# First block of an attention and GeGLU kernel: one statistic, one normalisation, one copy and the order of the up products

## The chip, the cores and the metric

The kernel runs on one core of one Trainium2 chip. The metric is the device time of one execution in microseconds (us). A core has TensorE (PE in the profile; PEld is its weight load), VectorE (DVE), ScalarE (ACT), GpSimd (POOL) and SyncE (SP, which here only issues transfers).

## The reference

```python
xn = layernorm(x)                                   # x: 1 x 2048 x 448, bf16
q, k, v = split(xn @ wqkv)                          # 16 heads of 28
p = softmax(mask(q @ k.T * 28 ** -0.5))             # causal, the last 256 positions
attn = (p @ v) @ wo
ffn  = (gelu_tanh(xn @ w_gate) * (xn @ w_up)) @ w_down    # inner width 1792
out  = x + attn + ffn
```

## The kernel before

The 2048 rows are 16 tiles of 128, worked on in four blocks (qb = 0 to 3) of four tiles. A block has an attention stage of steps (eight in the first block, two for each of four groups of four heads), then a stage that computes the gate products with Gelu. The program's order on each engine is written out by hand: every engine runs its own instructions in the order in which the Python code issues them, and waits for others by semaphores. A step of attention is: scores on TensorE (L680) into the score buffer, of which there is one, four PSUM banks large; the Exp of the whole buffer on ScalarE (L685, 1.88 us); masking; and then a list of other work, `plan[i]`, that is issued behind the step. At steps 4 and 6 the product with v of groups 0 and 1 (`pv`, L654) is issued ahead of the scores; it takes two PSUM banks `ov`, which ScalarE copies (L637) and VectorE adds to (L639).

The other four PSUM banks (b0 to b3) are handed out from a list, `spare`: `take` takes the bank at its head, `give` puts a bank at its end when the instruction that empties it has been issued, and whoever takes the bank later waits for that instruction.

The pieces of work that matter here:

- `stat(t)` (L155, L156), VectorE: mean and variance of a tile. `rstd(t, n)` (L160, L161), ScalarE: reciprocal deviation of n tiles, two small instructions. `norm(t)` (L170), VectorE: the normalised tile; for tiles from 4 on it is two instructions, of 448 and 64 columns. `dma_transp(t)` (L184): a transposing transfer from SP's queue into `xnT`.
- `v_dense` and `v_half` compute v of a tile in the first block, `v_copy` (L234) brings it from PSUM to `v_sb`, on the engine that is passed to it.
- `gen_qk()` yields the q and k products of groups 1 to 3 of the first block, nine items: for a group, q, k, and a last item that adds the remaining 64 rows and casts q (L251, ScalarE) and k (L252, VectorE) to SBUF. Group 3's q is an item of its own behind group 2's k.
- `gen_up(0, (1, 2, 3, 0, 4), (2, 3, 4))` (L497) computes the up products of five pairs of the first block's feed-forward part ahead of time: a pair is seven items (chunks of the contraction) of two matmuls each into two banks `ue`; behind the last item both are copied to `hT` (L514), both on VectorE, or for pairs 2, 3 and 4 the second on ScalarE. It reads `xsw`, the other half order of `xnT`, and `wu`.
- `gen_pairs(1, ...)` computes v (L331) and q and k (L345) of the second block. It needs `xnT` of tiles 4 to 7, `wvs` (loaded at L808), `xsw` of tiles 4 to 7 (`swap`, L478, a transfer from `xnT`: tiles 4 and 5 in one pair of transfers, tiles 6 and 7 in another) and `wsq` (`swap_weights`, L484).
- `masked` (L611), GpSimd, masks the first four steps; `fill_pads` (L295 to L307), GpSimd, fills columns of the weights which `swap_weights` then copies. `scale_o` (L620) runs on GpSimd, too.

`(u, 3)` in a plan means three items of the generator `u = chain(gen_qk(), gen_up(...))`, 44 items in all: nine of q and k, 35 of up products. The plan's first steps and what they call:

```python
def ahead():          # behind step 0
    norm(4); dma_transp(4)
    # two loads of wvs, SP's queue
def ahead2():         # within step 1
    stat(6); stat(7); rstd(5, 3)
def ahead3():         # within step 2
    for t in (5, 6, 7): norm(t); dma_transp(t)
    swap(1, 4, 2); fill_pads(False); swap_weights(); swap(1, 6, 2)
    # loads of wg, wu, x_sb, wo, wd
plan = [[last_v, (u, 3), ahead], [(u, 2), ahead2, (u, 2)], [(u, 1), ahead3, (u, 7)], [(u, 10), lambda: stat(8)],
        [lambda: stat(9), (u, 11), lambda: fill_pads(True)], [(u, 8), "sums"], ...]
```

So step 0's three items are group 1's q and k and their casts; step 1 holds group 2's q, k, group 3's q and group 2's casts; step 2 holds group 3's k and casts and six of the seven chunks of the first pair. Step 3 (ten items) ends the first pair, does the second, and begins the third with two chunks. `rstd(4, 1)` has been issued long before, ahead of step 0. Ahead of step 0 come also the v copies: `v_copy(0)` on ScalarE, `v_copy(1)` and `v_copy(3)` on VectorE; `last_v` computes v of tile 2 and copies it on VectorE.

Of the kernel before, what the change touches and what calls it, by code (L numbers as in the profile page):

```python
# [27 lines left out]
def kernel(  # L28
# [11 lines left out]
    nc = tc.nc  # L40
# [112 lines left out]
    def stat(t):  # L153
        st = work.tile([P, nc.vector.BN_STATS_DIM], f32, name="st")
        nc.vector.bn_stats(out=st[:, :], in_=x_sb[:, t, :])  # L155
        nc.vector.bn_aggr(out=mv_all[:, t, :], in_=st[:, :])  # L156

    def rstd(t, n):
        lnv = work.tile([P, 4], f32, name="lnv")
        nc.scalar.activation(out=lnv[:, 0:n], in_=mv_all[:, t:t + n, 1], func=ACT.Ln, bias=eps_t[:, 0:1], scale=1.0)  # L160
        nc.scalar.activation(out=rstd_all[:, t:t + n], in_=lnv[:, 0:n], func=ACT.Exp, scale=-0.5)  # L161
# [3 lines left out]
    def norm(t):  # L165
        xn = work.tile([P, 4, P], bf16, name="xn", bufs=4)
        xf = xn[:, :, :].rearrange("p a b -> p (a b)")
        both = ((0, D, 0), (D, 64, 384))
        for lo, n, src in both if t > 3 else both[:1]:
            nc.vector.tensor_scalar(out=xf[:, lo:lo + n], in0=x_sb[:, t, src:src + n], scalar1=mv_all[:, t, 0:1],  # L170
                                    scalar2=rstd_all[:, t:t + 1], op0=ALU.subtract, op1=ALU.mult)
        xns[t] = xn
# [9 lines left out]
    def dma_transp(t):  # L182

        nc.sync.dma_start_transpose(out=xnT[:, :, t * P:(t + 1) * P], in_=xns.pop(t)[:, :, :].rearrange("p a b -> p (a b)"))  # L184
# [26 lines left out]
    def take(name, cols=QB, tag=None):  # L211

        tag = tag or spare[0]
        spare.remove(tag)
        ps = psum.tile([P, QB], f32, name=name, tag=tag, bufs=1)[:, 0:cols]
        held[id(ps)] = tag, ps
        return ps  # L220

    def give(*tiles):
        for ps in tiles:
            spare.append(held.pop(id(ps))[0])


    def v_dense(t, pv, first=True):
        mm3(pv, lambda c: xnT[:, c, t * P:(t + 1) * P], lambda c: wv[:, c, :], first, not first)
# [4 lines left out]
    def v_copy(t, pv, copy):  # L233
        copy(out=v_sb[:, t, :, 0:Dh], in_=pv.rearrange("p (h d) -> p h d", d=Dh))  # L234
        give(pv)
# [52 lines left out]
    def fill_pads(last):  # L288


        def put(dst, src, n, lo):

            src = src.rearrange("p (j d) -> p j d", d=Dh)[:, :, lo:]
            if n == 4:
                nc.gpsimd.tensor_copy(out=dst[:, 12:16, Dh:32], in_=src[:, :, 24:28])  # L295
            src = src[:, :, 0:24].rearrange("p j (g i) -> p g j i", i=8)[:, :, :, 0:4]
            nc.gpsimd.tensor_copy(out=dst[:, 0:12, Dh:32].rearrange("p (g j) i -> p g j i", j=4), in_=src)

        if not last:
            for c in range(3):  # L300
                k = wraw[:, c, D + 12 * Dh:2 * D]
                put(wqp[:, c, :, :], k, 4, 0)
                put(wkp[:, c, :, :], k, 3, 4)
            return
        put(w3p[0:64, :, :], w3k[0:64, :], 4, 0)
        put(w3p[64:128, :, :], w3k[64:128, :], 3, 4)
        nc.gpsimd.memset(w3p[64:128, 12:16, :], 0.0)  # L307
# [161 lines left out]
    def new_hT(qb):  # L469
        hT = blk.tile([P, NF, QB], bf16, name="hT", tag="hT")  # L470
        hTs[qb] = hT
# [269 lines left out]
    def pads(eng, dst, gs):  # L741

        hs = slice(4 * gs.start, 4 * gs.stop)
        c0 = D * (dst is wkp)
        src = wraw[:, 0:3, c0 + Dh * hs.start:c0 + Dh * hs.stop]
        eng(out=dst[:, :, hs, 0:Dh], in_=src.rearrange("p c (h d) -> p c h d", d=Dh))
# [20 lines left out]
    pvs = [take("pv", D)]  # L767
# [25 lines left out]
    qk_copies(0, 0, pq, pk)  # L793
    pads(nc.vector.tensor_copy, wqp, slice(1, 2))
    v_copy(0, pvs[0], nc.scalar.copy)
    v_copy(1, pvs[1], nc.vector.tensor_copy)
    pads(nc.vector.tensor_copy, wkp, slice(1, 2))
    v_dense(3, pvs[3], False)
    v_copy(3, pvs[3], nc.vector.tensor_copy)
# [1 line left out]
        pads(nc.vector.tensor_copy, dst, slice(2, 4))  # L801

    def ahead():
        norm(4)
        dma_transp(4)
        wv64 = A_wqkv[0:3 * P, 2 * D:3 * D].rearrange("(c h p) n -> h p c n", h=2, p=64)
        for hi in range(2):
            nc.sync.dma_start(out=wvs[64 * hi:64 * hi + 64, :, :], in_=wv64[1 - hi])  # L808

    def ahead2():  # L810
        stat(6)
        stat(7)
        rstd(5, 3)

    def ahead3():
        for t in (5, 6, 7):
# [18 lines left out]
    for qb in range(NB):  # L835
        if qb in (1, 3):
            tc.mark_branch_hint_location("general", hint="LikelyTaken",
                                         engines=[mybir.EngineType.DVE if qb == 1 else mybir.EngineType.PE])
        early = ()
        if qb == 0:  # L840
            new_hT(0)
            early = (0, 1, 2, 3, 4)
            def last_v():
                v_dense(2, pvs[2], False)
                v_copy(2, pvs[2], nc.vector.tensor_copy)

            u = chain(gen_qk(), gen_up(0, (1, 2, 3, 0, 4), (2, 3, 4)))
            w = gen_pairs(1, (("v", 0), ("v", 2), ("k", 0), ("k", 1), ("k", 2)))
            plan = [[last_v, (u, 3), ahead], [(u, 2), ahead2, (u, 2)], [(u, 1), ahead3, (u, 7)], [(u, 10), lambda: stat(8)],
                    [lambda: stat(9), (u, 11), lambda: fill_pads(True)], [(u, 8), "sums"],  # L850
                    [(w, 7), "inverse", "scale", (w, 7), lambda: stat(10), (w, 3)],
                    [(w, 4), lambda: stat(11), lambda: rstd(8, 4), (w, 7), "masks", "sums", (w, 7), "inverse"]]
        else:
            d = gen_down(qb - 1)
            if qb < 3:
                u = gen_pairs(qb + 1, (("v", 0), ("k", 0), ("v", 2), ("k", 1), ("k", 2)))
                plan = [[(d, 14)], [(d, 11)], [(d, 11)], [(u, 7)], [(d, 17)], ["sums", (d, 1), (u, 7), "inverse"], [(u, 11)],
                        [lambda: q_last(qb + 1, nc.vector.tensor_copy), (d, 6), "sums"], [(d, 2), "inverse", (d, 9)],
                        [(u, 9), "masks", (u, 1)]]
                plan[3] = [(d, 1), (u, 7)]  # L860
                if qb == 2:
                    plan[0], plan[2] = [(d, 13)], [(d, 10)]
                if qb == 1:
                    for i, j in enumerate((0, 1, 2, 2)):
                        plan[j].insert(0, lambda t=12 + i: stat(t))
                    plan[4].append(lambda: rstd(12, 4))
                    plan[1] = plan[1][:1] + [lambda: q_last(1, nc.vector.tensor_copy), (d, 8)]
                    plan[2] = plan[2][:2] + [(d, 12), lambda: collect(1)]
                    plan[4].append(lambda: deliver(1))
            else:  # L870
                new_hT(3)
                early = (1, 2, 3, 4, 5, 6)
                u = gen_up(3, early, (4, 5, 6))
                plan = [[(u, 12)], [(u, 9)], [(d, 12)], [(d, 10)], [(d, 12)], [(d, 1), (u, 7), "sums"], [(d, 12), "inverse"],
                        ["sums", "inverse", (d, 11)], [(d, 11)], [(d, 1), "masks", (u, 13), "masks", (u, 1)]]
        if qb in (1, 2):
            swap(qb + 1)
        score_pool(1)
        rest, after, flush = attention(qb, plan)
        nc.scalar.preload_act_table(ACT.Gelu_apprx_tanh)  # L880
        score_pool(2)
        if qb not in hTs:
            new_hT(qb)

        def hook(f):
            after(f)
            if qb in (1, 2) and f == 0:
                collect(qb + 1)
            if f == (8, 2, 2, 0)[qb]:
                o_collect(qb, nc.sync if qb else nc.scalar)  # L890
            if f == (12, 4, 4, 0)[qb]:
                o_deliver(qb)
                o_finish(qb)
            if qb == 0 and f == 6:
                nc.gpsimd.tensor_copy(out=wo[64:128, 3, :], in_=wo[0:64, 3, :])
            if qb in (1, 2) and f == 10:
                deliver(qb + 1)
            t = ({0: 8, 4: 9, 8: 10, 10: 11} if qb == 0 else {4: 12, 6: 13, 8: 14, 10: 15} if qb == 1 else {}).get(f)
            if t is not None:
                norm(t)  # L900
                dma_transp(t)

        gated(qb, early, rest, flush, hook)
        if qb < NB - 1:
            nc.scalar.preload_act_table_set("natural_log_exp_and_others")
# [159 lines left out]
```

## Time and profile before

| | |
|---|---|
| median of 3 runs | 212.45 us (212.22 to 212.5) |
| profiled execution | 212.49 us, of which span 210.7 us |
| granted TensorE clock | 1.0 |
| busy: PE, DVE, ACT, POOL | 205.3, 156.7, 134.2, 43.9 us |
| Exp of attention (L685) | 38 of 1.879 us |
| first block, scores of step 0 | 11.28 us from the span's start |
| first block, scores of step 7 | 32.82 us |

Times in a timeline are microseconds from the start of the span. A row gives the start, the duration, the engine, the line of the kernel, the operation, what is written and read, and the count when several instructions are drawn together; in brackets stands how long the engine had been idle and which instruction released it. A matmul's duration contains its pipeline, so that matmuls overlap in the rows, and the pace is read from their starts; some records of matmuls are missing. SP's rows are the issuing of transfers, not their landing.

### The profile page before, as it was taken

What the parts mean: (1) busy time and instruction counts of PE and PEld (TensorE: products, weight loads), DVE (VectorE), ACT (ScalarE), POOL (GpSimd) and SP (SyncE); (2) the same over time, 40 slices, a digit from 0 to 9 for tenths busy, and PEclk for the clock granted to TensorE, in tenths of its full rate; (3) what the DMA queues carried; (4) which work ended last, traced back from release to release, by engine and by line L of the source; (5) the groups of instructions that cost most, each with busy time, mean ns of one, the idle gap of its engine ahead of it and who ended that gap; (6) DMA issues with size and microseconds to landing.
All of it is one profiled execution on the core that took longest, in us unless ns stands there. A gap on an engine that the chain in (4) does not pass through costs nothing. (4 is left out here: it accounts for less than half of the span.)

```text
span 210.7 us, 6666 instructions
## 1 busy us (share of the span) xinstructions
PE 205.3 (97%) x2837; PEld 99.5 (47%) x2842; DVE 156.7 (74%) x360; ACT 134.2 (64%) x131; POOL 43.9 (21%) x87
## 2 busy tenths in 40 slices
PE   7999999999999999999999999999999999999994
PEld 2444454544444445444445444544444454544572
DVE  6899889899788985696538897395385699696532
ACT  4688896966777977413778688623587787756000
POOL 5388912260000220040000112013000023042000
PEclk9999999999999999999999999999999999999999
DMA  6999979969411001003331000100000010100011
GB/s 186 282 228 164 132 189 228 249 193 230 110 46 49 25 0 41 10 0 68 62 91 47 25 3 23 23 3 19 24 5 0 3 47 5 44 11 14 3 47 50
DMA packets 24890, 15.68 MB, mean 74 GB/s; under 512 B 9208, under 2 KB 24728, under 8 KB 24856
## 3 DMA queue, kind: packets, MB, share of 16 engines
q1 hardware_dynamic: 23814, 14.87, 31.8%
q10 hardware_dynamic: 1042, 0.34, 1.0%
q8 instruction: 23, 0.38, 0.7%
q14 instruction: 11, 0.09, 0.3%
HBM read 9.26 MB, written 2.41 MB: 55 GB/s over the span
## 5 line engine op out<-in xcount | busy, mean ns | idle before, releaser
L685 ACT ACTIVATE p_sb<-sc 128x2048 bf16<-128x2048 f32 x38 | 71.4, 1879 | 17.0 <-PE sc L680 11.4
L537 ACT ACTIVATE p_sb<-gt 128x1024 bf16<-128x1024 f32 x28 | 28.7, 1025 | 31.3 <-PE gt L497 29.7
L620 POOL TENSOR_TENSOR oN<-oc,l 128x512 bf16<-128x512 f32 x16 | 20.7, 1300 | 122.9 <-DVE l L633 122.9
L497 PE MATMUL gt<-xnT,wg 64*128 64x512 bf16 x224 | 45.6, 376 | 0.0
L406 PE MATMUL po<-wd,hT 128*128 128x448 bf16 (+1 forms) x224 | 44.7, 347 | 0.0
L497 PE MATMUL gt<-xsw,wg 64*128 64x512 bf16 x168 | 40.7, 376 | 0.0
L605 DVE TENSOR_TENSOR p_sb<-p_sb,masks 128x256 bf16<-128x256 bf16 (+1 forms) x98 | 30.5, 365 | 7.5 <-ACT p_sb L685 7.5
L547 DVE TENSOR_TENSOR hT<-p_sb,u 128x512 bf16<-128x512 bf16 x34 | 21.7, 675 | 13.3 <-PE u L497 13.3
L406 PEld LDWEIGHTS <-hT 128*128 128x128 bf16 x238 | 21.9, 98 | 19.1 <-issue 2.0
L497 PEld LDWEIGHTS <-wg 64*128 64x128 bf16 x392 | 19.1, 94 | 22.3
L497 PEld LDWEIGHTS <-wu 64*128 64x128 bf16 x392 | 19.2, 94 | 21.9 <-issue 0.7
L497 PE MATMUL u<-xnT,wu 64*128 64x512 bf16 x136 | 28.1, 376 | 0.0
L497 PE MATMUL u<-xsw,wu 64*128 64x512 bf16 x102 | 24.7, 376 | 0.0
L639 DVE TENSOR_TENSOR oc<-oc,ov 128x512 f32<-128x512 f32 (+1 forms) x16 | 10.5, 658 | 10.4 <-ACT oc L637 10.2
L497 PE MATMUL ue<-xnT,wu 64*128 64x512 bf16 x88 | 18.1, 377 | 0.0
L680 PE MATMUL sc<-qT,kT 28*64 28x320 bf16 (+4 forms) x736 | 16.2, 259 | 0.2 <-ACT p_sb L685 0.2
L497 PE MATMUL ue<-xsw,wu 64*128 64x512 bf16 x66 | 16.2, 376 | 0.0
L680 PEld LDWEIGHTS <-kT 28*64 28x64 bf16 x736 | 8.2, 103 | 12.4 <-issue 11.2
L394 DVE TENSOR_TENSOR res<-po,x_sb 128x448 bf16<-128x448 f32 (+1 forms) x14 | 8.1, 605 | 7.9 <-PE po L406 6.7
L514 DVE CAST hT<-ue 128x512 bf16<-128x512 f32 x16 | 10.5, 685 | 2.4 <-PE ue L497 2.4
L637 ACT COPY oc<-ov 128x512 f32<-128x512 f32 x16 | 9.4, 586 | 4.4 <-PE ov L654 4.4
L633 DVE STREAM_TRANSPOSE l<-inv_all 128x512 f32<-128x512 f32 x16 | 11.1, 701 | 0.1
(112 smaller groups left out, 279.9 us busy)
## 6 DMA issues: line engine op xcount, KB each, us to landing
out_dram<-res SPq DMA_DIRECT2D x15, 112.0 KB
wd<-in_B_w_down_dram SPq DMA_DIRECT2D x2, 784.0 KB
x_sb<-in_A_x_dram SPq DMA_DIRECT2D x3, 448.0 KB
xsw<-xnT SPq DMA_DIRECT2D x6, 192.0 KB
wu<-in_B_w_up_dram SPq DMA_DIRECT2D x4, 224.0 KB
wg<-in_B_w_gate_dram SPq DMA_DIRECT2D x2, 448.0 KB
wu<-in_B_w_up_dram SPq DMA_DIRECT2D x2, 336.0 KB
wg<-in_B_w_gate_dram SPq DMA_DIRECT2D x2, 336.0 KB
```

The lines of the kernel that those rows point to most:

```text
L406: nc.tensor.matmul(po[:, 0:w], lhsT=x[:, k, tt * P:(tt + 1) * P], rhs=wt[:, k, lo:up], start=start and n == 0, stop=stop and n == len(term ...
L497: nc.tensor.matmul(ps, lhsT=w[64 * hi:64 * hi + 64, c, p * P:(p + 1) * P], rhs=xchunk(qb, hi, c, qb * QB, QB), start=c == 0, stop=c == 6, ...
L514: copy(out=hTs[qb][:, p + 7 * i, :], in_=us[i])
L537: nc.scalar.activation(out=ges[p][:, :, :], in_=gt[:, :, :], func=ACT.Gelu_apprx_tanh)
L547: nc.vector.tensor_tensor(out=hT[:, p + 7 * i, :], in0=ge[:, i, :], in1=u, op=ALU.mult)
L605: nc.vector.tensor_tensor(out=reg, in0=reg, in1=m, op=ALU.mult)
L620: nc.gpsimd.tensor_tensor(out=oN[:, g, :], in0=oc[:, :], in1=inv, op=ALU.mult)
L633: nc.vector.transpose(out=l1[:, :, :], in_=inv_all[:, 4 * qb + g, :].unsqueeze(2).to_broadcast([P, 16, 32]))
L637: nc.scalar.copy(out=oc[:, :], in_=ov[0][:, :])
L639: nc.vector.tensor_tensor(out=oc[:, q0:], in0=oc[:, q0:], in1=ov[1][:, q0:], op=ALU.add)
L680: nc.tensor.matmul(ss[k0:k0 + nk, j, col:col + nq], lhsT=kT[r, g, kt * P + k0:kt * P + k0 + nk], rhs=qT[r, g, ring(qb).start + q0:ring(qb) ...
L685: nc.scalar.activation(out=p_sb[:, :, 0:ncol], in_=ss[:, :, 0:ncol], func=ACT.Exp, scale=SCALE)
```

## The change

Three things of the first block are moved, and one goes to another engine.

- `v_copy(1)` runs on ScalarE instead of VectorE.
- `stat(6)` is issued behind `last_v` in step 0, ahead of group 1's k cast, instead of in step 1.
- `norm(4)` and `dma_transp(4)` are issued in step 1 behind `rstd(5, 3)`, instead of behind group 1's casts in step 0. The two loads of `wvs` keep their place in step 0, and so come ahead of tile 4's transpose in SP's queue.
- The up products are dealt out as 8, 12 and 9 items to steps 3, 4 and 5 instead of 10, 11 and 8: step 3 ends with the second pair complete, step 4 holds the third pair and five chunks of the fourth, step 5 the rest.

```diff
     v_copy(0, pvs[0], nc.scalar.copy)
-    v_copy(1, pvs[1], nc.vector.tensor_copy)
+    v_copy(1, pvs[1], nc.scalar.copy)
...
     def ahead():
-        norm(4)
-        dma_transp(4)
         wv64 = A_wqkv[0:3 * P, 2 * D:3 * D].rearrange("(c h p) n -> h p c n", h=2, p=64)
         for hi in range(2):
             nc.sync.dma_start(out=wvs[64 * hi:64 * hi + 64, :, :], in_=wv64[1 - hi])

     def ahead2():
-        stat(6)
         stat(7)
         rstd(5, 3)
+        norm(4)
+        dma_transp(4)
...
-            plan = [[last_v, (u, 3), ahead], [(u, 2), ahead2, (u, 2)], [(u, 1), ahead3, (u, 7)], [(u, 10), lambda: stat(8)],
-                    [lambda: stat(9), (u, 11), lambda: fill_pads(True)], [(u, 8), "sums"],
+            plan = [[last_v, lambda: stat(6), (u, 3), ahead], [(u, 2), ahead2, (u, 2)], [(u, 1), ahead3, (u, 7)], [(u, 8), lambda: stat(8)],
+                    [lambda: stat(9), (u, 12), lambda: fill_pads(True)], [(u, 9), "sums"],
```

## The prediction

> **What bounds the kernel now.** I read the page first, then the timelines of TensorE, ScalarE, VectorE and the SP queue over the first 31 us, then the table of stretches for the transfers. On the page:
>
> ```profile
> PE   7999999999999999999999999999999999999994
> ```
>
> This is TensorE's busy share in 40 slices: nines in all but the first and the last. So only a gap that TensorE has can be won, and whatever closes one moves all that follows. A nine hides up to a tenth of a slice, some 0.5 us, and such gaps lie in the first block. TensorE's timeline (start, duration, and in brackets idle time and releaser):
>
> ```profile
> 17.76 0.39 PE L204 MATMUL pk<-xnT,w3p 64*128 64x512 bf16 x1
> 18.08 0.37 PE L497 MATMUL ue<-xnT,wu 64*128 64x512 bf16 x1
> ...
> 19.25 0.38 PE L497 MATMUL ue<-xnT,wu 64*128 64x512 bf16 x1
> 19.86 0.43 PE L680 MATMUL sc<-qT,kT 28*64 28x320 bf16 x24 [0.23 <-ACT p_sb L685]
> 20.22 0.60 PE L497 MATMUL ue<-xnT,wu 64*128 64x512 bf16 x3
> ...
> 22.20 0.37 PE L497 MATMUL ue<-xnT,wu 64*128 64x512 bf16 x1
> 22.90 0.62 PE L654 MATMUL ov<-p_sb,v_sb 64*32 64x320 bf16 x36 [0.33 <-DVE hT L514]
> ...
> 25.99 0.38 PE L497 MATMUL ue<-xnT,wu 64*128 64x512 bf16 x1
> 26.29 0.43 PE L680 MATMUL sc<-qT,kT 28*64 28x320 bf16 x24
> ...
> 30.75 0.51 PE L331 MATMUL pv<-wvs,xsw 64*128 64x448 bf16 x2
> ```
>
> The undisturbed step from a last up product to the next scores is 25.99 to 26.29, 0.30 us. The two disturbed ones are 19.25 to 19.86 (0.61 us, released by the Exp) and 22.20 to 22.90 (0.70 us, released by an hT copy). The excess, 0.31 and 0.40 us, is lost; the bracket shows less, since ends of matmuls are modelled. A third loss is small. Ten pairs of up products start between 20.22 and 22.20, nine steps of 0.22 us; a pair of halves, as narrow, costs the same, so the first up product could follow the q and k halves at 17.76 + 0.22 = 17.98, but starts at 18.08.
>
> What holds the Exp of step 2 is on ScalarE:
>
> ```profile
> 4.88 0.20 ACT L161 ACTIVATE rstd_all<-lnv 128x1 f32<-128x1 f32 x1
> ...
> 10.81 0.54 ACT L234 CAST v_sb<-pv 128x448 bf16<-128x448 f32 x1
> 11.82 1.88 ACT L685 ACTIVATE p_sb<-sc 128x2048 bf16<-128x2048 f32 x1 [0.47 <-DVE v_sb L234]
> ...
> 14.51 1.88 ACT L685 ACTIVATE p_sb<-sc 128x2048 bf16<-128x2048 f32 x1
> 17.02 0.30 ACT L160 ACTIVATE lnv<-mv_all,eps_t 128x3 f32<-128x3 f32 x1 [0.63 <-DVE mv_all L156]
> ...
> 17.46 0.57 ACT L251 CAST qT<-pq 128x512 bf16<-128x512 f32 x1
> 17.92 1.88 ACT L685 ACTIVATE p_sb<-sc 128x2048 bf16<-128x2048 f32 x1
> ...
> 20.40 1.88 ACT L685 ACTIVATE p_sb<-sc 128x2048 bf16<-128x2048 f32 x1
> ```
>
> The Exp of step 1 ends at 14.51 + 1.88 = 16.39, but the reciprocal deviation of tiles 5 to 7 waits 0.63 us for VectorE's statistics; behind it stand group 2's q cast (17.46, over at 18.03: the bank which the first up product at 18.08 takes) and the Exp of step 2 (17.92 to 19.80: what the scores at 19.86 wait for, as the scores have one buffer). VectorE in the same time:
>
> ```profile
> 4.43 0.36 DVE L170 TENSOR_SCALAR xn<-x_sb,mv_all,rstd_all 128x448 bf16<-128x448 bf16 x1
> ...
> 11.15 0.61 DVE L234 CAST v_sb<-pv 128x448 bf16<-128x448 f32 x1
> ...
> 13.02 0.60 DVE L234 CAST v_sb<-pv 128x448 bf16<-128x448 f32 x1
> 14.06 0.69 DVE L252 CAST kT<-pk 128x512 bf16<-128x512 f32 x1 [0.44 <-PE pk L204]
> 14.67 0.85 DVE L170 TENSOR_SCALAR xn<-x_sb,mv_all,rstd_all 128x448 bf16<-128x448 bf16 x2
> 15.43 0.61 DVE L155 BATCH_NORM_STATS2 st<-x_sb 128x6 f32<-128x448 bf16 x1
> ...
> 16.80 0.18 DVE L156 BATCH_NORM_AGGREGATE mv_all<-st 128x2 f32<-128x6 f32 x1
> 16.90 0.66 DVE L252 CAST kT<-pk 128x512 bf16<-128x512 f32 x1
> 17.59 2.10 DVE L170 TENSOR_SCALAR xn<-x_sb,mv_all,rstd_all 128x448 bf16<-128x448 bf16 x6
> 19.61 0.68 DVE L252 CAST kT<-pk 128x512 bf16<-128x512 f32 x1
> 20.64 1.29 DVE L514 CAST hT<-ue 128x512 bf16<-128x512 f32 x2 [0.36 <-PE ue L497]
> ```
>
> It idles 0.44 us ahead of group 1's k cast (14.06), then normalises tile 4 (0.85) and takes the statistics of tiles 6 and 7 from 15.43 to 16.98, 0.78 each. These rows carry the first loss.
>
> **The change, part by part.**
>
> *A v copy to ScalarE.* VectorE loses 0.61 us of work (11.15), some 0.52 between starts, so its queue reaches the v copy of 13.02 at about 12.5, and is free at 13.1 instead of 13.62; that copy's product has by then been done, or it costs at most the 0.44 us of the hole. ScalarE gains an equal of the copy at 10.81, 0.54 us, from 11.25 to 11.79. The Exp of step 0 starts at 11.82 because its scores come then, so the copy lies in that hole: cost nothing, at most 0.05; without the cover 0.45, but TensorE does not wait for this Exp by itself.
>
> *Statistics of tile 6 ahead of group 1's k cast.* One statistic, 0.78 us, into 13.1 to 14.06: fits, by 0.18 us. If it didn't, the k cast would slip by up to 0.3, and the scores that need it come at step 2, over 2 us later; cost nothing.
>
> *Tile 4 behind tile 7.* VectorE goes k cast (to 14.75), statistics of tile 7 (to 15.45), tile 4 (0.85, to 16.3), and is free when group 2's k cast comes (16.90 before, about 16.8 now). So the statistics are in at 15.45, a microsecond before the Exp of step 1 ends. ScalarE then runs from 16.39 without a wait: the two small steps take 17.46 − 17.02 = 0.44, the q cast 0.46, so the Exp of step 2 starts at 17.3, 0.62 sooner, and ends at 19.2. The first up product comes at 17.98 (gain 0.10), the scores of step 3 at 19.25 − 0.10 + 0.30 = 19.45 without waiting (gain 0.31). What is late next there is TensorE itself. Tiles 5 to 7 start some 0.14 sooner, as the k cast, not the deviation, now frees VectorE.
>
> *Up products by pairs.* Two chunks leave step 3, of which one goes to step 4 and one more to step 5 (10, 11, 8 become 8, 12, 9): 44 in both orders, nothing added. Step 3 now ends with the second pair whole and the third not begun, so the banks at the head of the spare list for pv(0) are those of the first pair, not those whose copies begin when TensorE wants them. The loss of 0.40 goes, if the first pair's copies are over. They ran 20.64 to 21.93; 0.41 sooner they end at 21.52, if group 3's k cast (19.61 to 20.29, now 0.14 sooner) is out by 20.23, which is tight by less than 0.1. TensorE arrives at 22.90 − 0.40 − 0.41 − 2 × 0.22 = 21.65. I take 0.06 off for this hand-over, and 0 to 0.3 as its bounds. The scores of step 4 follow after pv(0)'s 0.55, at 22.2, and need the Exp of step 3: it starts 0.54 after its scores (19.86 to 20.40), so now at 20.0, and ends at 21.9, 0.3 in time.
>
> *The queue of SP.* Tile 4's transpose moves behind the two wvs loads:
>
> ```profile
> 15.55 1.32 SPq L184 DMA_TRANSPOSE xnT<-xn  x1
> 16.93 1.26 SPq L808 DMA_DIRECT2D wvs<-in_A_wqkv_dram  x2
> 18.45 4.30 SPq L184 DMA_TRANSPOSE xnT<-xn  x3
> 24.14 1.85 SPq L478 DMA_DIRECT2D xsw<-xnT  x2
> ...
> 27.40 1.28 SPq L478 DMA_DIRECT2D xsw<-xnT  x2
> ```
>
> ```profile
> 19.00:20.00 1.00, 0.78 (x15) 0.37 (x19) 1.00 (x4) 1.00 (x2) 0.28 (x2) 1.00 0.13 15
> 20.00:21.00 1.00, 1.00 (x32) 0.64 (x21) 0.64 (x2) 0.88 (x2) 1.00 (x3) 1.00 0.61 147
> ...
> 29.00:30.00 1.00, 1.00 (x44) 0.58 (x25) 0.97 (x3) 1.00 (x3) 0.00 (x0) 1.00 0.83 202
> 30.00:31.00 1.00, 1.00 (x14) 0.68 (x12) 1.00 (x4) 1.00 (x1) 0.00 (x0) 1.00 0.46 78
> ```
>
> The last column of the table is GB/s of all transfers. The wvs loads read an input and wait for no engine: they went out as soon as the transpose ahead of them was issued (15.55 + 1.32 = 16.87). Now they leave before 16.3; the transpose leaves at 16.3 instead of 15.55, 0.75 later, with nothing behind it until tile 5's at about 18.3. The stake lies further on. The swap copies of tiles 6 and 7 go out at 27.40 to 28.68 and the second v product needs them at 30.75. TensorE would be there at 30.75 − 0.75 = 30.0. The transfers' landing has no row; its bounds are 28.68 and 30.75, and as the queues still move 202 GB/s in 29 to 30 and 78 in the next microsecond I take 30.4. So without a shift of this chain TensorE would wait 0.45 there. The chain starts with the swap at 24.14, released by the transposes. Now the transfers were all but idle at 19 to 20 (15 GB/s), with tile 4's transpose and wvs both issued, and at 147 in the next microsecond: something held wvs until then, and what stood ahead of it was the transpose. With wvs gone ahead, that hole is used, tiles 4 to 7 go back to back, and the swap may leave up to 24.14 − 22.75 = 1.39 sooner, when SP has issued the last transpose. I take about 1; 0.45 is enough. The Trainium skill's "DMA: Bandwidth & Descriptors", section "Queues, rings and completion order", says that each engine takes its descriptors in ring order. By it the loads that now stand in front delay tile 4's transpose, while tile 5's, behind both in either order, is not later; the trace agrees as far as wvs, issued second, was held.
>
> *Sum.* 0.10 + 0.31 + 0.40 − 0.06 = 0.75 us. The profiled execution took 212.49 us (span 210.7, the rest around it), 0.04 over the median of 212.45: 212.49 − 0.75 − 0.04 = 211.7 us. From 31 us on every stage follows TensorE, so the gain stays. Bounds of the sum: 0.50 (hand-over late by 0.3) to 1.0, were small waits of ScalarE and VectorE to go as well.
>
> **Rivals.** *The swap chain does not move* (the first transpose was slow of itself, not its neighbours): TensorE waits 0.45 for the second v product, the gain shrinks to 0.30, 212.2 us. For it: what gates the transfers at 19 to 20 is not shown. Against it: tile 5's issue and POOL's work are earlier in any case.
>
> *Slower: the four transposes move as a train with tile 4.* If tile 5's data wait for tile 4's, as wvs seems to have done, and tile 4's take as long from issue as before, all land up to 0.75 later; the second v product starts at 30.4 + 0.75 = 31.2 instead of 30.75: 0.45 us slower, 212.9 us. It decides from a delay of 0.35, beyond which nothing is won. Against it: 2.9 us lay between the issues of tiles 4 and 5, and 2 remain.
>
> *The change does not do what it says:* tile 4's normalisation waits for the deviation step now issued ahead of it, which writes the same small tile. Then VectorE stands until 16.85, group 2's k cast ends at 18.4, and the first pair's copies at 22.4; pv(0) would wait as long as before: 212.5. Against it: the norm at 4.43 ran ahead of the deviation written at 4.88, another column of that tile.
>
> *Hand-over late by 0.25 in all:* 211.95.
>
> **How the numbers follow.** A measurement tells about 0.2%, 0.42 us, from no change: faster is below 212.03, slower above 212.87. Forecast 0.60, late hand-over 0.06: faster 0.66. Swap chain unmoved 0.16, no effect 0.04: same 0.20. Train 0.12 and other slips 0.02: slower 0.14. The forecast's own range is 211.4 to 212.0 by its bounds; to hold 8 in 10 it reaches on over the unmoved chain and the case of no effect, to 212.6, and leaves the train out.
>
> **What would show it.** ScalarE: no wait before the deviation of tiles 5 to 7, Exp of step 2 near 17.3. TensorE: scores of step 3 near 19.45 and pv(0) near 21.65, neither with a bracket over 0.1; second v product near 30.0. SP: the swap copies before 23.7. Wrong if the second v product's wait shows on TensorE, if pv(0) waits on hT copies again, or if the transposes' train reaches past 24.14.

## The result, and the profile after

The changed kernel takes 211.75 us in the median (211.62 to 212.07, 8 runs) against 212.43 us before (8 runs): a ratio of 0.9968, with a 95% interval of 0.9957 to 0.9979, or 0.68 us gained (0.45 to 0.91). The forecast was 211.7 us, a gain of 0.75. Three executions of e3 and two of g3 below took 3 to 4 us longer than the others; they are left out of the ratios, and the one of e3 that is profiled is among them.

One thing has to be known before the traces are laid side by side. The scores of step 0 come at 11.57 us here and came at 11.28 before, though nothing ahead of them was changed; in the executions profiled for this document they come between 11.22 and 11.95. The spans (210.2 and 210.7) therefore differ by less than the kernels do. I read distances from the scores of step 0 instead. TensorE's timeline after:

```profile
11.57 0.42 PE L680 MATMUL sc<-qT,kT 28*64 28x320 bf16 x16
...
18.06 0.39 PE L204 MATMUL pk<-xnT,w3p 64*128 64x512 bf16 x1
18.28 0.38 PE L497 MATMUL ue<-xnT,wu 64*128 64x512 bf16 x1
18.28 0.59 PE L497 MATMUL ue<-xsw,wu 64*128 64x512 bf16 x2
...
19.36 0.38 PE L497 MATMUL ue<-xnT,wu 64*128 64x512 bf16 x1
19.67 0.43 PE L680 MATMUL sc<-qT,kT 28*64 28x320 bf16 x24
20.03 0.60 PE L497 MATMUL ue<-xnT,wu 64*128 64x512 bf16 x3
20.39 0.46 PE L497 MATMUL ue<-xsw,wu 64*128 64x512 bf16 x2
...
21.47 0.59 PE L497 MATMUL ue<-xnT,wu 64*128 64x512 bf16 x3
21.99 0.62 PE L654 MATMUL ov<-p_sb,v_sb 64*32 64x320 bf16 x36
...
30.27 0.51 PE L331 MATMUL pv<-wvs,xsw 64*128 64x448 bf16 x2
...
32.33 0.43 PE L680 MATMUL sc<-qT,kT 28*64 28x320 bf16 x24
```

From 11.57 to 32.33 (scores of step 7) are 20.76 us; before it was 32.82 − 11.28 = 21.54: 0.78 gained in this stretch, and the rest of the kernel follows. The three gaps are seen closing one by one. The first up product follows the halves after 0.22 us (18.06 to 18.28; before 0.32). The scores of step 3 follow the last up product after 0.31 (19.36 to 19.67; before 0.61), without a bracket. pv(0) comes at 21.99 without a bracket; the row of 21.47 holds three matmuls, the last of them some 0.22 later, and from there to 21.99 is 0.30 (before 0.70). A new gap is in between: after the chunk of 20.03 the second pair's second half starts at 20.39 instead of 0.22 later, at 20.25.

One gain more is in these rows. After, the first pair's second half starts together with its first half (18.28 both); before, it started 0.10 behind it (18.08 and 18.18):

```profile
18.18 0.49 PE L497 MATMUL ue<-xsw,wu 64*128 64x512 bf16 x2
```

So the last up product ahead of step 3 comes 19.36 − 11.57 = 7.79 us behind the scores of step 0 instead of 19.25 − 11.28 = 7.97, which is 0.18 sooner, where 0.10 was forecast.

ScalarE's timeline after:

```profile
14.80 1.88 ACT L685 ACTIVATE p_sb<-sc 128x2048 bf16<-128x2048 f32 x1
16.57 0.30 ACT L160 ACTIVATE lnv<-mv_all,eps_t 128x3 f32<-128x3 f32 x1
...
17.05 0.58 ACT L251 CAST qT<-pq 128x512 bf16<-128x512 f32 x1
17.53 1.88 ACT L685 ACTIVATE p_sb<-sc 128x2048 bf16<-128x2048 f32 x1
```

ScalarE's deviation step has lost its bracket: it follows the Exp of step 1 at once (16.57), and the Exp of step 2 starts at 17.53 instead of 17.92, or 5.96 us behind the scores of step 0 instead of 6.64.

VectorE's timeline after:

```profile
13.33 0.62 DVE L155 BATCH_NORM_STATS2 st<-x_sb 128x6 f32<-128x448 bf16 x1
...
14.35 0.69 DVE L252 CAST kT<-pk 128x512 bf16<-128x512 f32 x1 [0.18 <-PE pk L204]
...
15.61 0.18 DVE L156 BATCH_NORM_AGGREGATE mv_all<-st 128x2 f32<-128x6 f32 x1
15.71 0.68 DVE L170 TENSOR_SCALAR xn<-x_sb,mv_all,rstd_all 128x448 bf16<-128x448 bf16 x2
17.08 0.69 DVE L252 CAST kT<-pk 128x512 bf16<-128x512 f32 x1 [0.70 <-PE pk L204]
17.69 2.06 DVE L170 TENSOR_SCALAR xn<-x_sb,mv_all,rstd_all 128x448 bf16<-128x448 bf16 x6
19.66 0.68 DVE L252 CAST kT<-pk 128x512 bf16<-128x512 f32 x1
20.45 1.29 DVE L514 CAST hT<-ue 128x512 bf16<-128x512 f32 x2
```

VectorE idles 0.18 us, not 0.44, ahead of group 1's k cast, with tile 6's statistic in the hole; tile 7's is over at 15.79, and tile 4's normalisation at 16.39 has time to spare before group 2's k cast. Group 3's k cast ends at 19.66 + 0.68 = 20.34: the up product of 20.39 takes that cast's bank, and this is what it waited for. SP's queue after, and behind it one row of the table of stretches (last column: GB/s of all transfers):

```profile
14.31 1.26 SPq L806 DMA_DIRECT2D wvs<-in_A_wqkv_dram  x2
16.41 5.82 SPq L184 DMA_TRANSPOSE xnT<-xn  x4
22.78 1.29 SPq L478 DMA_DIRECT2D xsw<-xnT  x2
...
25.97 1.28 SPq L478 DMA_DIRECT2D xsw<-xnT  x2
```

```profile
19.00:20.00 1.00, 1.00 (x32) 0.41 (x28) 1.00 (x3) 0.89 (x2) 0.94 (x3) 1.00 2.15 195
```

The swaps leave at 22.78 and 25.97 instead of 24.14 and 27.40. In the microsecond from 19 the transfers move 195 GB/s; before it was 15.

### The profile page after: what moved, and what is told of

Same layout as the page of the kernel before. It is cut to its first block, busy times and chain, and to the rows that moved or that the text cites. A ratio compares the mean times of both kernels' runs of the same rounds, so it can differ in the third digit from the quotient of the medians.

```text
span 210.2 us, 6672 instructions
## 1 busy us (share of the span) xinstructions
PE 205.6 (98%) x2842; PEld 99.5 (47%) x2842; DVE 156.5 (74%) x359; ACT 134.9 (64%) x132; POOL 43.7 (21%) x87
```

## The experiments

The stretch from the scores of step 0 to those of step 7 comes from the one profiled execution of each; the ratio is against the kernel before on the same chip.

| kernel | stretch, us | ratio to before, 95% interval |
|---|---|---|
| before | 21.54 | 1 |
| after | 20.76 | 0.9968 (0.9957 to 0.9979) |
| e1: after, up products as before | 21.31 | 0.9979 (0.9970 to 0.9989) |
| e2: before, up products by pairs | 21.11 | 0.9981 (0.9973 to 0.9990) |
| e3: after, wvs behind tile 4's transpose | see below | 0.9972 (0.9963 to 0.9981) |
| e4: after, group 3's casts ahead of tile 7 | 20.63 | 0.9960 (0.9945 to 0.9974) |
| f1: after, tile 4 back in step 0 | 21.00 | 0.9972 (0.9946 to 0.9999) |
| f2: after, v copy back on VectorE | 20.94 | 0.9962 (0.9940 to 0.9983) |
| f3: before, tile 4 moved, no more | 21.06 | 0.9971 (0.9949 to 0.9992) |
| f4: before, wvs ahead, no more | 21.55 | 0.9996 (0.9975 to 1.0018) |
| g1: after, again | 20.77 | 0.9974 (0.9964 to 0.9984) |
| g2: e4, again | 20.64 | 0.9958 (0.9944 to 0.9971) |
| g3: e4 without the copy and the early statistic | 20.66 | 0.9957 (0.9942 to 0.9972) |

**e1, the up products as before.**

```diff
-  ..., (u, 8), lambda: stat(8)], [..., (u, 12), ...], [(u, 9), "sums"]
+  ..., (u, 10), lambda: stat(8)], [..., (u, 11), ...], [(u, 8), "sums"]
```

> The changed kernel with the up products dealt out as before (10, 11, 8). Theory (the two gaps of TensorE add up): step 3's scores stay near 19.7 us, but pv(0) again takes the banks of the second pair, whose copies begin when TensorE wants them, so about 0.40 us comes back: 212.15 us, with a bracket on pv(0) that names the hT copy. Rival (once ScalarE's wait is gone VectorE is ahead, and the order of the pairs is worth nothing): 211.75 us, no bracket on pv(0).

TensorE's timeline of e1:

```profile
19.38 0.43 PE L680 MATMUL sc<-qT,kT 28*64 28x320 bf16 x24
19.74 0.60 PE L497 MATMUL ue<-xnT,wu 64*128 64x512 bf16 x3
20.36 0.39 PE L497 MATMUL ue<-xsw,wu 64*128 64x512 bf16 x2
...
22.09 0.38 PE L497 MATMUL ue<-xnT,wu 64*128 64x512 bf16 x1
22.62 0.65 PE L654 MATMUL ov<-p_sb,v_sb 64*32 64x320 bf16 x36 [0.16 <-DVE hT L514]
```

The Exp no longer holds step 3's scores (19.38, 8.10 behind those of step 0, as after), but pv(0) has its bracket with the hT copy again. The time gives back 0.23 us of the 0.68 (0.9979 against 0.9968), the stretch 0.55. The stretch loses more than the forecast 0.40: pv(0) is late by 22.62 − 22.09 − 0.30 = 0.23, and the second pair's second half is late by 20.36 − 19.74 − 0.22 = 0.40, not by 0.14. That second part, 0.26, isn't shown to come from the order of the up products: nothing ahead of that half differs from the changed kernel, and VectorE's normalising instructions ahead of it took longer in this execution (see f1). f3 below, which lacks the pairs as well, is 0.30 behind the changed kernel. The times leave it open, since the two intervals overlap.

**e2, the up products by pairs alone**, the diff of e1 the other way round, on the kernel before.

> The kernel before, with nothing but the up products dealt out by pairs (8, 12, 9). Theory: the Exp of step 2 still waits for the statistics, step 3's scores stay some 0.3 to 0.4 us late, but pv(0) follows the last up product after 0.3 us instead of 0.7: about 0.4 us gained, 212.0 us. Rival (the first pair's copies on VectorE, behind group 3's k cast, hold pv(0) in their turn, as they are not moved up here): no gain, 212.4 us.

TensorE's timeline of e2:

```profile
19.57 0.38 PE L497 MATMUL ue<-xnT,wu 64*128 64x512 bf16 x1
20.17 0.43 PE L680 MATMUL sc<-qT,kT 28*64 28x320 bf16 x24 [0.23 <-ACT p_sb L685]
...
21.84 0.59 PE L497 MATMUL ue<-xnT,wu 64*128 64x512 bf16 x3
22.36 0.62 PE L654 MATMUL ov<-p_sb,v_sb 64*32 64x320 bf16 x36
```

Step 3's scores wait for the Exp as before (19.57 to 20.17), pv(0) does not wait: the row of 21.84 holds three matmuls, so the last starts 0.30 before 22.36. The stretch is shorter by 0.43, the time by 0.19% or 0.40 us.

So the two causes stand apart: in the stretch the statistics alone give 0.48 (f3 below, by tile 4's move) and the pairs alone 0.43, together 0.78. The 0.13 short of the sum is about the size of the new wait at the second pair's bank, 0.14. In e2 it doesn't arise (the second half follows after 0.23, 20.53 to 20.76 in its trace), and in f3 it lies ahead of a wait of pv(0) that is there anyway. The times (0.45 in e1, 0.40 in e2, 0.68 together) are too coarse to tell.

**e4, group 3's casts first.**

```diff
-  [(u, 1), ahead3, (u, 7)]                  # ahead3: tiles 5, 6, 7, transfers
+  [(u, 1), ahead3, (u, 1), ahead4, (u, 6)]  # ahead3: tiles 5, 6; ahead4: tile 7, transfers
```

> The changed kernel with group 3's q and k casts ahead of tile 7's normalisation (step 2: one item, tiles 5 and 6, one item, tile 7 and the transfers, six items). In the trace after, the second pair of up products starts its second half 0.14 us late, just when group 3's k cast on VectorE is over, whose bank it takes. Theory: that wait goes, 0.14 us gained, 211.6 us, and the swap copies leave as early as after. Rival (VectorE gets to the first pair's copies no sooner, so pv(0) waits for those instead): 211.75 us. Rival on the other side: tile 7's transpose is late by 0.6 us, and with it the swap copies; 211.75 us as they have over a microsecond to spare.

TensorE's and VectorE's timelines of e4:

```profile
20.10 0.60 PE L497 MATMUL ue<-xnT,wu 64*128 64x512 bf16 x3
20.33 0.59 PE L497 MATMUL ue<-xsw,wu 64*128 64x512 bf16 x2
...
21.93 0.62 PE L654 MATMUL ov<-p_sb,v_sb 64*32 64x320 bf16 x36
```

```profile
17.76 1.30 DVE L170 TENSOR_SCALAR xn<-x_sb,mv_all,rstd_all 128x448 bf16<-128x448 bf16 x4
18.96 0.68 DVE L252 CAST kT<-pk 128x512 bf16<-128x512 f32 x1
...
20.52 1.29 DVE L514 CAST hT<-ue 128x512 bf16<-128x512 f32 x2 [0.25 <-PE ue L497]
```

The cast ends at 19.64, and the second pair goes on at the plain pace (20.10 to 20.33). pv(0) follows without a wait though the first pair's copies end no sooner than at 21.81. The stretch is 20.63, 0.13 below after, and in the same two kernels again, g2 and g1, it is 20.64 against 20.77; both times the ratio is the lower one (0.9960 and 0.9958 against 0.9968 and 0.9974), though the intervals overlap.

> The changed kernel itself, for a comparison on the same chip with the next two: 0.7 us below the kernel before, 20.8 us from the scores of step 0 to those of step 7.

> The changed kernel with group 3's casts ahead of tile 7's normalisation, again, beside the changed kernel. Theory: the pair's bank no longer waits for VectorE: 20.63 us from step 0's to step 7's scores, 0.85 us below the kernel before, 0.15 below the changed kernel. Rival (a difference of one execution): no less than the changed kernel.

**f1, f2 and f3: which edit frees ScalarE.** f1 puts the two lines of tile 4 back ahead of the wvs loads, f2 gives `v_copy(1)` back to VectorE, both on the changed kernel; f3 moves the two lines of tile 4 behind `rstd(5, 3)` in the kernel before, and nothing else.

> The changed kernel with tile 4's normalisation and transpose back in step 0, ahead of the wvs loads; tile 6's statistic stays early. Theory: with that statistic early the other one is over at about 16.4, just as ScalarE comes to it, so the Exp of step 2 still starts near 17.3 and TensorE keeps both gains; only the transfers stand as before, and what they cost is seen alone: 0 to 0.45 us, 211.75 to 212.2 us. Rival (the statistics need both moves to be in time): ScalarE waits again, step 3's scores late by 0.3, 212.1 us.

> The changed kernel with the v copy of tile 1 back on VectorE. Theory (the copy's place is worth nothing): group 1's k cast slips by 0.3 to 0.4 us, the statistics of tile 7 are over by 16.1 instead of 15.8, still ahead of ScalarE, 211.75 us. Rival (the copy buys the slot for tile 6's statistic, and without it the chain is late): step 2's Exp late by 0.3, about 212.0 us.

> The kernel before with nothing but tile 4's normalisation and transpose moved behind tile 7's statistic. Theory: this alone takes 0.85 us out from between group 1's k cast and the two statistics, which are over at 16.2, ahead of the Exp of step 1; ScalarE's wait goes, step 3's scores come near 19.4, 0.40 us gained, 212.05 us, as with all but the pairs. Rival (it takes the early statistic as well): half of it, 212.25 us.

ScalarE's timelines of f1 and of f3:

```profile
14.61 1.88 ACT L685 ACTIVATE p_sb<-sc 128x2048 bf16<-128x2048 f32 x1
16.37 0.30 ACT L160 ACTIVATE lnv<-mv_all,eps_t 128x3 f32<-128x3 f32 x1
...
17.34 1.88 ACT L685 ACTIVATE p_sb<-sc 128x2048 bf16<-128x2048 f32 x1
```

```profile
15.18 1.88 ACT L685 ACTIVATE p_sb<-sc 128x2048 bf16<-128x2048 f32 x1
16.95 0.30 ACT L160 ACTIVATE lnv<-mv_all,eps_t 128x3 f32<-128x3 f32 x1
...
17.91 1.88 ACT L685 ACTIVATE p_sb<-sc 128x2048 bf16<-128x2048 f32 x1
```

In all three the deviation follows the Exp of step 1 with no bracket and step 3's scores come 8.09 or 8.10 us behind those of step 0, as after. So tile 4's move frees ScalarE by itself (f3), and the early statistic does so without tile 4's move (f1, with the v copy on ScalarE). Once tile 4 is moved, the v copy isn't needed (f2, f3); the early statistic alone, without the copy and without tile 4's move, was not run. f3's stretch is 0.48 below the kernel before, where 0.40 was expected. What f1 and f2 lose in the stretch, 0.24 and 0.18, they lose at the second pair's bank. VectorE in f1:

```profile
17.50 2.30 DVE L170 TENSOR_SCALAR xn<-x_sb,mv_all,rstd_all 128x448 bf16<-128x448 bf16 x6
19.70 0.68 DVE L252 CAST kT<-pk 128x512 bf16<-128x512 f32 x1
```

The six instructions of tiles 5 to 7 take 2.30 us here (2.25 in f2, 2.32 in e1; 2.06 after), which makes group 3's k cast late by as much. As e1 shows such a long time with nothing changed ahead of it, this loss needn't come from the edits of f1 and f2. In the times it doesn't show: 0.9972 and 0.9962, with intervals wide enough for either.

**f4 and e3: the place of the wvs loads.**

```diff
 def ahead():                 # f4, on the kernel before
+    (two loads of wvs)
     norm(4); dma_transp(4)
-    (two loads of wvs)
 def ahead2():                # e3, on the changed kernel; its ahead() is empty
     ...
     norm(4); dma_transp(4)
+    (two loads of wvs)
```

> The kernel before with nothing but the two wvs loads issued ahead of tile 4's transpose. Theory: the swap leaves about a microsecond sooner than at 24.1, but TensorE in this kernel does not wait for it, so no gain: 212.45 us. Rival (the swap copies hold TensorE a little in the kernel before, in executions without a profile too): 0.1 to 0.3 us gained, 212.2 us.

> The changed kernel with the two wvs loads issued behind tile 4's transpose instead of ahead of it; all engines' own orders unchanged. Theory (the place of wvs in the queue sets when the swap copies leave): the transfers stand nearly still while the first transpose is under way, wvs follows it, the first swap leaves near 24 us instead of 22.8, and TensorE waits 0.4 to 0.7 us at the second v product: 212.15 to 212.45 us. Rival (the first transpose is slow of itself, and what stands ahead of it does not matter): swap leaves at about 22.8 to 23.3 us, no wait at the second v product, 211.75 us.

In f4 the swaps leave at 22.80 and 26.67 instead of 24.14 and 27.40, and the time is the same: in the kernel before, TensorE does not wait for them. In e3's profiled execution, of 216.13 us, they leave at 25.17 and 27.85, and TensorE waits:

```profile
29.64 0.70 PE L331 MATMUL pv<-wv,xnT 64*128 64x448 bf16 x4
32.91 0.36 PE L331 MATMUL pv<-wvs,xsw 64*128 64x448 bf16 x2 [2.57 <-DMA xsw<-xnT]
```

TensorE stood 2.57 us for the swap of tiles 6 and 7, at the second v product. The late issue alone doesn't account for it: from the end of the issue (27.85 + 1.28 = 29.13) to TensorE's start are 3.78 us, where g2's second swap, issued from 26.70 to 27.98, had landed by 29.80, within 1.82. The executions that are compared don't show such a wait: 0.9972, where after has 0.9968. So the expected cost of 0.4 to 0.7 us was not found in them, and whether a little of it is there stays open: the two intervals would hide 0.2 us.

**g3, three edits only.** e4 without `v_copy(1)` on ScalarE and without the early statistic.

> Only three edits on the kernel before: tile 4 behind tile 7's statistic, the up products by pairs, and group 3's casts ahead of tile 7's normalisation; the v copy stays on VectorE and tile 6's statistic in step 1. Theory (the copy and the early statistic carry nothing): as the one before, 20.65 us between the two scores, 0.85 us below the kernel before. Rival (VectorE, with 0.5 us more of work ahead, is late for group 2's k cast and all behind it): 0.1 to 0.3 us of it lost.

It keeps the gain: 20.66, 0.9957. No part of it is seen to come from the copy or the early statistic.

## Why the prediction was right

Its steps came out nearly one by one, counted from the scores of step 0. The Exp of step 2: forecast 17.3 − 11.28 = 6.02, measured 5.96. The scores of step 3: forecast 8.17, measured 8.10. pv(0): forecast 10.37, measured 10.42. The second v product: forecast 30.0 − 11.28 = 18.72, measured 30.27 − 11.57 = 18.70. The terms 0.31 and 0.40 are seen in the rows (0.61 became 0.31, and 0.70 became 0.30), and f3 and e2 show the statistics and the pairs apart.

*Two terms were mis-sized, and cancel.* The first term, 0.10, measured 0.18: the prediction counted the late first half of the first pair and not that its second half was 0.10 later still. Both delays go together with ScalarE's wait (e1 and f3 lack them, e2 and f4 have them); what held the second half is not shown. The hand-over was put at 0.06 and cost 0.14. So 0.18 + 0.31 + 0.40 − 0.14 is 0.75 again, and that part of the agreement is luck.

*The hand-over came at another place.* VectorE's k cast of group 3 was named as what could be late, and was. The prediction held it against the first pair's copies and so against pv(0); it held back the second pair's second half, which takes that cast's bank. The prediction followed the spare list for pv(0) and not for the pair before it. e4 shows it: cast sooner, wait gone, the first pair's copies where they were, pv(0) not late.

*What was costed at nothing was worth nothing*, and more than was said: f3 and g3 show that the v copy and the early statistic, for which room was reckoned (0.18 us to spare forecast, 0.18 idle measured), aren't needed for the gain. Tile 4's move frees ScalarE alone, since 0.85 us come out from between the k cast and the statistics, and 0.63 had to. The prediction took the moves as one and never asked which of them the wait needed.

*The rivals.* The slower one, the transposes moving as a train with tile 4, did not come: the swaps left earlier, not later. Neither did the unmoved chain. What it would have cost stays open, as it rested on a landing at 30.4 that no row showed. e1 has the same head as before and its second swap leaves at the same 27.40; its second v product starts at 30.53 without a wait, which rules out a later landing and not one at 30.4.

The cause that was given for the earlier swap, wvs held behind the transpose, is not shown. f4 changes that order alone, and its first swap leaves 22.80 − 11.22 = 11.58 us behind the scores of step 0, against 24.14 − 11.28 = 12.86 before. But e2 and f1 keep the old order, and there it leaves at 11.86 in both, with 82 and 144 GB/s in the microsecond from 19 instead of 15. Two executions of one kernel, e4 and g2, have it at 11.23 and 12.27. So single executions differ by a microsecond with the order unchanged, as much as the prediction put on the change of order. The Trainium skill's page "DMA: Bandwidth & Descriptors", "Queues, rings and completion order", has each engine take its descriptors in ring order; that by itself says nothing of how long the transfers stood at 19 to 20.

The last rival did not come either: the deviation step that writes beside tile 4's column did not hold its normalisation, which starts at 15.71 in the trace after, with the deviation at 16.57.

## What to carry to other kernels

When an engine's bracket names a releaser, ask what stands between that releaser's inputs and it in its own queue, and how little has to come out: here 0.63 us had to come out, either of two moves of 0.78 and 0.85 did it, and both were made. When work is dealt out by counts, the bank or buffer list decides who waits for whom, so follow it for every taker, not for the one whose wait is in view. And compare profiled executions from an instruction that both kernels reach alike: the spans differed by 0.5 us where the stretch showed 0.78. Before a shift in one trace is given a cause, look at a second execution of the same kernel: the swap's departure moved by a microsecond without any change.

## What was not expected of the hardware

The same six normalising instructions of VectorE took 2.06 to 2.32 us from one variant to the next. The changed kernel took 2.06, and 2.07 in g1; e1, with nothing changed ahead of them, took 2.32. What makes the difference was not tried. The head of the kernel, unchanged, varied by 0.7 us (11.22 to 11.95).

In e3's profiled execution the granted clock (the third column from the right in the table of stretches) falls after the stall of 2.57 us. It is 1.00 up to 33, the stall included, and then:

```profile
33.00:34.00 1.00, 1.00 (x11) 0.41 (x11) 0.00 (x0) 0.00 (x0) 0.04 (x1) 0.86 1.14 210
34.00:35.00 1.00, 1.00 (x8) 0.50 (x6) 0.38 (x1) 0.02 (x1) 0.00 (x0) 0.50 1.09 246
35.00:36.00 1.00, 1.00 (x6) 0.14 (x1) 0.97 (x4) 0.51 (x1) 0.00 (x0) 0.50 1.13 217
36.00:37.00 1.00, 1.00 (x27) 0.53 (x28) 0.50 (x2) 0.03 (x1) 0.00 (x0) 0.50 1.13 241
37.00:38.00 1.00, 1.00 (x10) 0.39 (x8) 0.01 (x1) 1.00 (x1) 0.00 (x0) 0.94 1.13 204
```

It is 0.86, then 0.50 for three microseconds, and back at 0.94 some four us later. The Trainium skill's page "TensorE: Matmul & The Clock Gate", section "Why this matters for your kernels", advises to keep idle gaps below about 3 us; here the fall followed a gap of 2.57 us. This is one execution, and no run shows that the gap was the cause.
